# A fused BigBird attention and expert layer on one core: SyncE waits in front of a transfer until most of its older ones have landed

## The chip, the core and the metric

The kernel runs on one core of a Trainium2 chip. The core has five engines that run side by side, each with an instruction queue of its own: TensorE (PE; its weight loads are listed apart as PEld), VectorE (DVE), ScalarE (ACT), GpSimd (POOL) and SyncE (SP). SP does no arithmetic here; it issues transfers, which the core's 16 DMA engines carry out. The metric is the time of one execution on the device in microseconds (us). Times before are the median of three runs. A trace was taken of one more execution; its span is the time from the first to the last recorded instruction.

## The reference

```python
def _attn_ref(q, k, v, sampled_blocks):          # 4 x 8 x 768 x 64, float32
    scores = scale * np.matmul(q, k.transpose(0, 1, 3, 2))
    mask = np.abs(blk_i - blk_j) <= window        # blocks of 32, window 1
    mask = mask | (blk_i == 0) | (blk_j == 0) | (blk_i == n_blocks - 1) | (blk_j == n_blocks - 1)
    for qb in range(n_blocks):
        for kb in sampled_blocks[qb]:             # 3 blocks drawn for each of 24
            mask[qb * block:(qb + 1) * block, kb * block:(kb + 1) * block] = True
    ...
    return np.matmul(attn, v)                     # attn: softmax of the masked scores

def _moe_ref(x, w_in, w_out):                     # 3072 x 512, 512 x 2048, 2048 x 512
    r = np.maximum(x @ w_in, 0.0)
    return (r * r) @ w_out

x = attn_out.transpose(0, 2, 1, 3).reshape(B * S, H * D)
out = _moe_ref(x, w_in, w_out)
```

Attention runs over four batches of eight heads with 768 tokens of 64 numbers. Each token sees its own block of 32, the neighbours, the first and last block, and three blocks drawn at random for its block. The result, 3072 rows of 512, goes through two products with a squared ReLU between them.

## The kernel before

Everything is computed in bf16 with sums in float32. Two heads make a unit, so a batch has four units. **Batches 0 and 1** compute all scores of a unit and multiply by a mask after the exponential. **Batches 2 and 3** (`b >= SB`) compute only what is seen: the queries are taken in visits of two groups, the keys of the drawn blocks are put together by copies (`k_gather`, tile `KG`) and the values are fetched by transfers from a copy of V in device memory (`v_store` writes tensor `rows`, `v_gather` and `v_window` read it into tile `VG`).

For each unit, Q and K are loaded in float32 (`load`, tiles `qs` and `ks`; in batches 0 and 1 as rows of 1536 bytes, in 2 and 3 Q and K as rows of 512 bytes), cast to bf16 (tile `qc`) by DVE or POOL, and turned by a transposing transfer into tile `QKT` (`transp_dma`), which PE reads for the scores. V is loaded (tile `vs`) and cast (tile `VB`). PE multiplies scores into cells of PSUM (`X`), ACT takes the exponential (tile `pT`), DVE masks, PE multiplies with V, DVE normalizes (tile `XS`), and a transposing transfer writes the turned result into tile `xT` (`x_transp_dma`, and `s_transp` in batches 2 and 3). PE multiplies `xT` by `w_in`, DVE, ACT and POOL take the squared ReLU (tiles `r` and `g`), PE multiplies by `w_out`, the result is copied to tile `ys` and stored (`store`).

Nothing here is ordered by a scheduler. About 1220 tasks are made first; then `PROGRAM`, a long string, is read word by word. A word is a letter for the engine (P, V, A, G, S) and the number of a task, and the task's instructions are put at the end of that engine's queue. An engine takes its queue in order. Words of all four batches are mixed, so PE works on the expert product of one batch beside the scores of the next.

SP issues 170 transfers, all on one hardware queue (q1 on the profile's page), in the order of the words that begin with S. Loads of weights and indirect gathers go over POOL's queue (q0). Every transfer of SP signals one of eight semaphores (DMAHW0 to DMAHW7 in the order of instructions), taken in turn, and waits until the transfer that used the same semaphore has landed, so at most eight are under way at once. In the code, SP's transfers are started through the name `sy`, which is `nc.sync`:

Of the kernel before, what the change touches and what calls it, by code (L numbers as in the profile page):

```python
# [12 lines left out]
F32 = mybir.dt.float32  # L13
# [12 lines left out]
def kernel(  # L26
# [11 lines left out]
    nc = tc.nc  # L38
    B, H, S, D = q.shape
# [8 lines left out]
    HP = H // 2  # L48
# [12 lines left out]
    SB, VR, KG_BUFS, VG_BUFS = 2, D + 2, 2, 3  # L61
# [12 lines left out]

    GATES = (4, 5)
    AHEAD = {(2, 4, 9): 2, (3, 0, 1): 0}
    HOLD = {586: 976, 563: 977, 564: 978, 542: 956}
    passed, held_by, last_pe = {}, [None], [None]
    HALVES = slice(0, D), slice(D, P)
    SYNC = mybir.DependencyInfo(mybir.DependencyClass.Sync, mybir.DependencyReason.DATA)  # L80
    MASKED = ((256, 512), (512, 768), (0, 256))
    FULL = (0, 256)
    tasks = []
    class Buf:
        def __init__(self, pool):
            self.pool, self.holds, self.at = pool, 0, None
# [9 lines left out]
    def run_program(bufs):  # L96
        names = {"P": "PE", "V": "DVE", "A": "ACT", "G": "POOL", "S": "SP"}
        taken = {name: [] for name in bufs}
        cells = [None] * NX
        for word in PROGRAM.split():  # L100
            t = tasks[int(word[1:].partition("/")[0])]
            if t.blocks and names[word[0]] in t.blocks[1]:
                wanted[names[word[0]]].append(t.blocks[0])
        for word in PROGRAM.split():
            i, _, spot = word[1:].partition("/")
            t = tasks[int(i)]
            assert not t.done and all(d.done for d in t.deps)
            for b in t.get:
                if b.pool == "X":
                    b.at = int(spot)  # L110
                    old, cells[b.at] = cells[b.at], b
                else:
                    b.at = len(taken[b.pool]) % bufs[b.pool]
                    taken[b.pool].append(b)
                    old = taken[b.pool][-1 - bufs[b.pool]] if len(taken[b.pool]) > bufs[b.pool] else None
                assert old is None or not old.holds
            held_by[0] = passed.get(HOLD.get(int(i)))
            t.fn(names[word[0]])
            passed[int(i)] = last_pe[0]
            t.done = True  # L120
            for b in t.put:
                b.holds -= 1
        assert all(t.done for t in tasks)
# [51 lines left out]
        eng.dma_start(out=raw[u][w][:, :, ns].rearrange("p t n d -> p t (n d)"),  # L175
                      in_=(qv, kv, vv)[w][0, u][:, :, ns.start * D:ns.stop * D])

    sy, sc_ = nc.sync, nc.scalar
    sb_i = consts.tile([nb, n_rand * 2], I32, name="sb_i")
    for eng, u, w, ns in ((sy, None, 0, ALL), (sc_, 0, 1, KEYS[0]), (sy, 0, 0, QRS[0]), (sc_, 0, 1, KEYS[1]), (None, 0, 0, ALL), (sy, 1, 0, QRS[0]),  # L180
                          (sy, 1, 1, ALL), (sy, 2, 0, QRS[0]), (sy, 2, 1, ALL), (sy, 0, 2, ALL), (sy, 3, 0, QRS[0]),
# [43 lines left out]
    col, row = blk[0:nb, 0:nb], blk[0:nb, nb:nb + 1]  # L225
# [346 lines left out]
    def load_blocks(e):  # L572
        if wanted[e]:
            held_at[e].append(blocks_of(wanted[e].pop(0), ENGINE[e]))
# [14 lines left out]
    def k_gather(b, v, g, e):  # L589
# [13 lines left out]
        for r_ in range(RS):  # L603
            eng.tensor_copy(out=rows[:, :, :, r_ * w:(r_ + 1) * w], in_=src[:, :, :, bass.ds(at[r_] * w, w)])  # L604
        for _ in range(AHEAD.get((b, v, g), 1)):
            load_blocks(e)
# [183 lines left out]
    def T_(f, *args, **kw):  # L790
        return Task((lambda e: f(*args, e)), **kw)
# [102 lines left out]
    def visit(b, v, vw, acts):  # L894
        gs_ = [g for g in VISITS[v] if g]
        vb, kb = Buf("vg"), Buf("kg")
        buf_of["vg", b, v] = vb
        cl = T_(v_claim, b, v, get=[vb], deps=mk_claims[-1:])
        parts = [T_(v_gather, b, v, i, deps=vw + [cl, tb["rows"], tb["slots"]]) for i, g in enumerate(VISITS[v]) if g]
        for t_, g in zip(parts, gs_):  # L900
            t_.blocks = g, ("SP",)
        parts.append(T_(v_window, b, v, deps=vw + [cl]))
        kc = {}
        for g in [g for g in VISITS[v] if g]:
            kc[g] = T_(k_gather, b, v, g, get=[] if kc else [kb], deps=[ev[u][1, 0] for u in us] + [tb["slots"], tb["rows"]] + list(kc.values()))
            kc[g].blocks = g, ("POOL", "DVE")
        slots, pts, exs = [], [], []
        for u, _, _, gs in acts:
            xb_, st, pt = Buf("X"), Buf("S"), Buf("pT")
            buf_of["pT", (u, v, gs)] = pt  # L910
            kgs = [kb] if gs[-1] else []
            sc = T_(s_scores, u, v, gs, xb_, deps=[ev[u][1, 0], ev[u][0, 0]] + [kc[g] for g in gs if g], get=[st, xb_], put=kgs)
            sc_of[u].append(sc)
            ex = T_(s_exps, u, v, gs, deps=[sc], get=[pt], put=[xb_, st])
            if gs[-1]:
                ex = T_(s_masks, u, v, gs, deps=[ex] + tb["masks"])
            exs.append(ex)
            pts.append(pt)
        yb, ot, xs = Buf("X"), Buf("po"), Buf("xs")
        va = T_(s_values, b, v, yb, deps=exs + parts + sum((cv[u] for u in us), []), get=[ot, yb], put=pts + [vb])  # L920
        for u in us:
            va_of[u].append(va)
        nm = T_(s_normalize, b, v, deps=[va], get=[xs], put=[yb, ot])
        mu["s", b, v] = T_(s_transp, b, v, deps=[nm] + x_get(b, v // 2 * QW), put=[xs])
# [4 lines left out]
    for i, (c0, c1) in enumerate(((0, QW), (QW, S))):  # L929
        rb_ = Buf("X")  # L930
        t = T_(mask_rows, c0, c1, rb_, get=[rb_])
# [10 lines left out]
    t = T_(table_load, deps=[])  # L942
# [4 lines left out]
    t = T_(table_spread, hb, deps=[tb["slots"]], get=[hb], put=tmp)  # L947
    tb["rows"] = T_(table_rows, deps=[t], put=[hb])
    m_ = [T_(table_masks, g0, g0 + n, deps=[t], put=[hb]) for g0, n in ((0, 6), (6, 5))]
    tb["masks"] = m_  # L950
    for us in [range(b * HP, (b + 1) * HP) for b in range(B)]:
        for u in us:
            prepare(u)
        mine = [a for a in order if a[0] in us]
        if us[0] < HP:
            for c0, c1 in MASKED:
                for n in range(0, NCH, 2):
                    mb = Buf("X")
                    t = T_(mask_tile, n, c0, c1, mb, get=[mb], deps=mr)
                    x = T_(mask_evac, n, c0, c1, deps=[t, mk_claims[[m_[0] for m_ in MASKED].index(c0)]], put=[mb])  # L960
                    for c in range(c0, c1, P):
                        mk[n, c] = mk[n + 1, c] = x
        if us[0] >= SB * HP:
            b = us[0] // HP
            vw = [T_(v_store, b, i, deps=sum((cv[u] for u in us), [])) for i in range(NVS)]
            for v in range(len(VISITS)):
                visit(b, v, vw, [a for a in mine if a[1] == v * P])
            continue
        for a in mine:
            attend(a, us[0] < HP and a[1] == 0)  # L970

    sq_of, gbuf = {}, {}
    for T in TILES:
# [21 lines left out]
        for i, y in enumerate(ys):  # L995
# [10 lines left out]
            yc0 = yc0 or [yc]  # L1006
            T_(store, T, i, y, deps=[yc], put=[ysb])

    PROGRAM = """
        V109 V153 V207 V332 V18 V19 V20 V28 V42 V53 V294 V29 A32 V35 P30/0 P36/1 P0/2 P33/3 V31 V37 A1 P11/0 V34 P100/1 G46  # L1010
        A101 P47/0 P104/2 V43 A105 P44/3 P102/1 V45 V57 V48 P58/2 A103 V54 P111/3 V59 P55/0 P113/2 A112 V56 P115/1 V41 P4/0
# [57 lines left out]
        P17/1 V1212 S1213  # L1069
    """  # L1070
    run_program({"y": 2, "S": 3, "H": 3, "po": 3, "pT": PT_BUFS, "r": R_BUFS, "g": G_BUFS, "ys": YS_BUFS, "qc": QC_BUFS, "xq": XQ_BUFS, "xT": XT_BUFS, "vg": VG_BUFS, "kg": KG_BUFS, "xs": 2, "qs": NRAW, "ks": NRAW - 1, "vs": NRAW - 1})


# [28 lines left out]
```

## Time and the profile before

| | us |
|---|---|
| runs before: median | 256.14 |
| runs before: lowest to highest | 256.11 to 257.24 |
| the profiled execution | 253.89 |
| its span in the trace | 252.1 |

| engine | busy us | instructions |
|---|---|---|
| PE (matmul) | 240.2 | 5265 |
| PEld (weight load) | 180.3 | 5265 |
| ACT | 184.4 | 217 |
| DVE | 164.6 | 386 |
| POOL | 96.5 | 199 |

The page gives the busy time of each engine, then the span in 40 slices, the queues of the DMA engines, the chain of work that ended last, and the costliest groups of instructions. Three lines of its 40 slices tell how the transfers are spread (each digit is a tenth of the slice, a 9 is 90% or more; a slice is 6.3 us):

```profile
PE   7788999999999999899999999899999999999994
...
DMA  6999999999899997999789999992615655242022
GB/s 187 363 291 177 200 246 206 241 254 245 182 276 226 233 243 227 148 271 163 215 235 239 204 203 208 254 270 57 177 30 87 160 156 133 78 127 83 3 86 86
```

PE is busy almost throughout. The DMA engines are full until slice 27, which ends at 170 us, and half empty after that.

### The profile page before, as it was taken

The numbers are of one execution on the slowest core, as the hardware profiler recorded it, in microseconds if no ns is written. First come the engines' busy times: TensorE is split into PE (matmuls) and PEld (weight loads), VectorE is DVE, ScalarE is ACT, GpSimd is POOL, SyncE is SP. The second block draws the span as 40 slices with busy tenths as digits, with TensorE's granted clock in tenths as the row PEclk, the third lists the DMA queues.
The fourth block names the chain that finished last, engine by engine and source line by source line (L and its number), as shares of the span: only waits on it lengthen the run. The fifth ranks groups of instructions, "written<-read, shape, count | busy, mean of one in ns | idle before, by whom it ended". The sixth has DMA issues, their size and how long they took to land.

```text
span 252.1 us, 12049 instructions
## 1 busy us (share of the span) xinstructions
PE 240.2 (95%) x5265; PEld 180.3 (72%) x5265; DVE 164.6 (65%) x386; ACT 184.4 (73%) x217; POOL 96.5 (38%) x199
## 2 busy tenths in 40 slices
PE   7788999999999999899999999899999999999994
PEld 4567889668965678777867776666966774776774
DVE  7668997779799989765653857626466568642300
ACT  3998999999998899868748676778697556225241
POOL 2265634010544014456566934053519306160020
PEclk9999999999999999999999999999999999999999
DMA  6999999999899997999789999992615655242022
GB/s 187 363 291 177 200 246 206 241 254 245 182 276 226 233 243 227 148 271 163 215 235 239 204 203 208 254 270 57 177 30 87 160 156 133 78 127 83 3 86 86
DMA packets 63540, 47.08 MB, mean 187 GB/s; under 512 B 31487, under 2 KB 58496, under 8 KB 63488
## 3 DMA queue, kind: packets, MB, share of 16 engines
q1 hardware_dynamic: 58352, 37.61, 65.2%
q0 software_dynamic: 4448, 8.25, 16.7%
q8 instruction: 41, 0.67, 1.2%
q10 hardware_dynamic: 688, 0.46, 0.6%
q14 instruction: 11, 0.09, 0.1%
HBM read 35.51 MB, written 7.91 MB: 172 GB/s over the span
## 4 chain that ended last, share of the span: by engine, by line
PE 85%; DMA 5%; DVE 4%; issue 2%; POOL 1%; ACT 1%; SPq 1%; DVEq 0%
PE X L209 78%; PE X L660 5%; DMA w_out_sb<-in_moe_w_out_dram 4%; DMA ks<-in_k_dram 2%; PE X L402 1%; DVE pT L371 1%; DVE r L716 1%; POOL g L727 1%; PE X L312 1%; DVE xq L417 1%; DVE qc L129 1%; ACT pT L364 0%; DVE QKT L129 0%; SPq L175 0%; PE X L431 0%
## 5 line engine op out<-in xcount | busy, mean ns | idle before, releaser
L209 PE MATMUL X<-xT,w_in_sb 64*128 64x256 bf16 x1536 | 99.1, 269 | 2.0 <-issue 1.5
L209 PE MATMUL X<-w_out_sb,g 64*128 64x512 bf16 (+3 forms) x960 | 94.6, 333 | 0.5 <-DMA w_out_sb<-in_moe_w_out_dram 0.5
L209 PEld LDWEIGHTS <-w_in_sb 64*128 64x128 bf16 x1536 | 73.5, 94 | 14.3 <-issue 2.6
L364 ACT ACTIVATE pT<-X 128x1024 bf16<-128x1024 f32 x72 | 70.7, 1033 | 6.8 <-PE X L209 5.2
L630 ACT ACTIVATE pT<-X 128x768 bf16<-128x768 f32 (+1 forms) x56 | 41.5, 765 | 25.9 <-PE X L209 24.3
L209 PEld LDWEIGHTS <-g 64*128 64x128 bf16 x960 | 40.5, 94 | 26.7 <-issue 0.6
L725 ACT ACTIVATE g<-r 128x1024 bf16<-128x1024 f32 (+1 forms) x44 | 40.3, 931 | 11.8 <-DVE r L716 11.7
L716 DVE TENSOR_SCALAR r<-X 128x1024 f32<-128x1024 f32 x22 | 26.9, 1223 | 25.1 <-PE X L209 23.6
L371 DVE TENSOR_TENSOR pT<-pT,VG 128x1024 bf16<-128x1024 bf16 x60 | 39.5, 697 | 1.6 <-ACT pT L364 1.4
L727 POOL TENSOR_TENSOR g<-r 128x512 bf16<-128x512 f32 (+1 forms) x16 | 20.7, 1305 | 47.9 <-ACT r L714 23.8
L637 DVE TENSOR_TENSOR pT<-pT,MKS 128x768 bf16<-128x768 bf16 (+1 forms) x48 | 28.3, 618 | 12.2 <-ACT pT L630 11.6
L714 ACT ACTIVATE r<-X 128x1024 f32<-128x1024 f32 x26 | 27.4, 1065 | 10.1 <-PE X L209 9.8
L209 PE MATMUL X<-QKT 64*128 64x256 bf16 (+1 forms) x384 | 31.4, 250 | 0.7 <-DVE QKT L129 0.4
L583 POOL DMA_INDIRECT VG<-rows,idx x20 | 20.3, 1015 | 26.2 <-PE X L209 11.9
L209 PEld LDWEIGHTS <-QKT 64*128 64x128 bf16 x384 | 17.0, 95 | 5.9 <-issue 1.5
L129 POOL CAST VB<-vs 128x768 bf16<-128x768 f32 x10 | 8.4, 847 | 25.6 <-DMA vs<-in_v_dram 24.1
L209 PEld LDWEIGHTS <-pT 64*128 64x128 bf16 x768 | 15.6, 94 | 2.9 <-PE X L209 0.2
L209 PE MATMUL X<-VB,pT 64*128 64x65 bf16 x768 | 17.1, 190 | 0.1
L129 POOL CAST qc<-ks 128x384 bf16<-128x384 f32 (+1 forms) x17 | 8.7, 541 | 20.6 <-DMA ks<-in_k_dram 14.1
L209 PEld LDWEIGHTS <-KG 64*128 64x128 bf16 x528 | 13.3, 95 | 4.2
L660 PEld LDWEIGHTS <-pT 128*64 128x64 bf16 x624 | 11.7, 111 | 4.9 <-issue 4.4
L604 POOL COPY KG<-QKT 128x64 int32 x72 | 15.0, 254 | 0.0
(104 smaller groups left out, 199.0 us busy)
## 6 DMA issues: line engine op xcount, KB each, us to landing
vs<-in_v_dram SPq DMA_DIRECT2D x14, 384.0 KB
ks<-in_k_dram SPq DMA_DIRECT2D x13, 384.0 KB
qs<-in_q_dram SPq DMA_DIRECT2D x12, 384.0 KB
out_dram<-ys SPq DMA_DIRECT2D x9, 512.0 KB
VG<-rows SPq DMA_DIRECT2D x20, 132.0 KB
w_in_sb<-in_moe_w_in_dram POOLq DMA_DIRECT2D x2, 1024.0 KB, 9.7
w_out_sb<-in_moe_w_out_dram POOLq DMA_DIRECT2D x4, 512.0 KB, 10.3
rows<-VB SPq DMA_DIRECT2D x4, 396.0 KB
```

What stands on the lines that cost most here:

```text
L129: (V if e == "DVE" else G).tensor_copy(out=out, in_=in_)
L209: last = nc.tensor.matmul(out(r ^ crossed), lhsT(r ^ crossed, rows), rhs(r ^ crossed, rows), skip_group_check=True, **kw)
L364: A.activation(out=pT[:, :, 0:n], in_=stile.pop(a)[:, :, 0:n], func=AF.Exp, scale=scale)
L371: V.tensor_tensor(out=pT, in0=pT, in1=m[:, None].broadcast_to([P, 2, len(cs), w]), op=AOP.mult)
L583: G.indirect_dma_start(out=to[0:RS * HB], out_offset=None, in_=pairs, in_offset=bass.IndirectOffsetOnAxis(ap=idx[0:RS * HB, g - 1:g], axis=0))
L630: A.activation(out=pT[:, :, 0:n], in_=stile.pop((u, v, gs))[:, :, 0:n], func=AF.Exp, scale=scale)
L637: V.tensor_tensor(out=pT, in0=pT, in1=m[:, None].broadcast_to([P, 2, n]), op=AOP.mult)
L660: nc.tensor.matmul(po[i * D:(i + 1) * D, h, a * VW:(a + 1) * VW], pts[g][:, h, c * D:(c + 1) * D], val, start=a == 0 and c == 0, stop=c == ...
L714: A.activation(out=to, in_=src, func=AF.Relu)
L716: V.tensor_scalar(out=to, in0=src, scalar1=0.0, scalar2=None, op0=AOP.max)
L725: A.activation(out=g, in_=r, func=AF.Square)
L727: (G if e == "POOL" else V).tensor_mul(out=g, in0=r, in1=r)
```

## The change

`sy` becomes an object that keeps a list of the transfers it has sent and their costs. The cost of a transfer is its number of rows times (`ROW_COST` + bytes of a row), with `ROW_COST` 1000. Ahead of each new transfer it counts back from the last one sent, as long as the sum of costs stays at or below `UNDER_WAY`, 1,900,000. What is older than that must have landed: SP gets a no-operation that waits for the landing of the newest of those older ones. This is switched on at the first word of SP whose task belongs to batch 2 or 3 (`third`), which is the 35th of SP's transfers, issued at 56 us in the trace before, and stays on. The order of tasks doesn't change, nor does any instruction of PE, DVE, ACT and POOL.

```diff
+    ROW_COST, UNDER_WAY = 1000, 1900000
...
+            sy.on = sy.on or (word[0] == 'S' and t in third)
             t.fn(names[word[0]])
...
-    sy, sc_ = nc.sync, nc.scalar
+    class Paced:
+        def __init__(self):
+            self.sent, self.landed, self.on = [], 0, False
+
+        def dma_start(self, out, in_, **kw):
+            row = (D * 2 if kw else in_.shape[-1]) * (4 if in_.dtype == F32 else 2)
+            cost = math.prod(in_.shape) // (D * 2 if kw else in_.shape[-1]) * (ROW_COST + row)
+            under_way, k = 0, len(self.sent)
+            while k > self.landed and under_way + self.sent[k - 1][1] <= UNDER_WAY:
+                k -= 1
+                under_way += self.sent[k][1]
+            if self.on and k > self.landed:
+                tc.add_manual_dep(nc.sync.nop().ins, self.sent[k - 1][0], SYNC, reason="little is under way when the next transfer begins")
+                self.landed = k
+            i = nc.sync.dma_start(out=out, in_=in_, **kw)
+            self.sent.append((i.ins.name, cost))
+            return i
+
+    sy, sc_ = Paced(), nc.scalar
...
+        if us[0] == SB * HP:
+            first = len(tasks)
...
+    third = set(tasks[first:])
```

The first place is SP's queue from 95 to 108 us of the trace before, between the load of a Q and the load of a V; a transfer is shown with what it writes and reads, and in brackets what it waits for. Before:

```order
L157 DMA qs_76<-in_q_dram 128x6x128 [waits DMAHW0_49]
L155 DMA vs_79<-in_v_dram 128x2x384 [waits DMAHW1_49,DVE_49]
L541 DMA rows_70<-VB_189 64x3168 [waits DMAHW2_49,Pool_49]
L541 DMA rows_70<-VB_189 64x3168 [waits DMAHW3_49]
L319 DMA_TRANSPOSE QKT<-qc_107 128x6x128 [waits DMAHW4_49,PE_49]
L319 DMA_TRANSPOSE QKT<-qc_109 128x6x128 [waits DMAHW5_49,PE_49,Pool_49]
L319 DMA_TRANSPOSE QKT<-qc_108 128x6x128 [waits DMAHW6_49]
L319 DMA_TRANSPOSE QKT<-qc_106 128x6x128 [waits DMAHW7_49,DVE_49]
L155 DMA vs_80<-in_v_dram 128x2x384 [waits DMAHW0_49]
```

The same rows of the change (all of SP's transfers have the line of the new class):

```order
L194 DMA qs_76<-in_q_dram 128x6x128 [waits DMAHW5_49,DMAHW0_49]
L194 DMA vs_79<-in_v_dram 128x2x384 [waits DMAHW1_49,DMAHW6_49,DVE_49]
L194 DMA rows_70<-VB_189 64x3168 [waits DMAHW2_49,DMAHW7_49,Pool_49]
L194 DMA rows_70<-VB_189 64x3168 [waits DMAHW0_49,DMAHW3_49]
L194 DMA_TRANSPOSE QKT<-qc_107 128x6x128 [waits DMAHW4_49,DMAHW1_49,PE_49]
L194 DMA_TRANSPOSE QKT<-qc_109 128x6x128 [waits PE_49,DMAHW5_49,DMAHW2_49,Pool_49]
L194 DMA_TRANSPOSE QKT<-qc_108 128x6x128 [waits DMAHW4_49,DMAHW6_49]
L194 DMA_TRANSPOSE QKT<-qc_106 128x6x128 [waits DMAHW7_49,DMAHW5_49,DVE_49]
L194 DMA vs_80<-in_v_dram 128x2x384 [waits DMAHW6_49,DMAHW0_49]
```

Nothing moves; every row has one semaphore more. The transfers of these rows signal DMAHW0 to DMAHW7 and then DMAHW0 again, in their order, so the transpose of `qc_108` now also waits for the landing of the one of `qc_107`, two rows above it.

The second place is SP's queue from 136 to 147 us of the trace before, transposes and loads for batch 3. Before:

```order
L319 DMA_TRANSPOSE QKT<-qc_108 128x6x128 [waits DMAHW4_49]
L157 DMA ks_78<-in_k_dram 128x6x128 [waits DMAHW5_49,Pool_49]
L319 DMA_TRANSPOSE QKT<-qc_106 128x6x128 [waits DMAHW6_49]
L157 DMA qs_76<-in_q_dram 128x6x128 [waits DMAHW7_49]
L319 DMA_TRANSPOSE QKT<-qc_109 128x6x128 [waits DMAHW0_49]
L673 DMA_TRANSPOSE xT_117<-XS 128x4x128 [waits DMAHW1_49,DVE_49]
L155 DMA vs_80<-in_v_dram 128x2x384 [waits DMAHW2_49]
```

And of the change:

```order
L194 DMA_TRANSPOSE QKT<-qc_108 128x6x128 [waits DMAHW0_49,DMAHW4_49]
L194 DMA ks_78<-in_k_dram 128x6x128 [waits DMAHW5_49,DMAHW1_49,Pool_49]
L194 DMA_TRANSPOSE QKT<-qc_106 128x6x128 [waits DMAHW4_49,DMAHW6_49]
L194 DMA qs_76<-in_q_dram 128x6x128 [waits DMAHW5_49,DMAHW7_49]
L194 DMA_TRANSPOSE QKT<-qc_109 128x6x128 [waits DMAHW6_49,DMAHW0_49]
L194 DMA_TRANSPOSE xT_117<-XS 128x4x128 [waits DMAHW1_49,DMAHW7_49,DVE_49]
L194 DMA vs_80<-in_v_dram 128x2x384 [waits DMAHW2_49]
```

From the third row on, each transfer but the last also waits for the landing of the one two rows above it; the load into `vs_80` keeps the wait it had.

## The prediction

> **What bounds the kernel now.** I read the page first: the busy shares, the table of DMA queues, and the shares of the chain that ended last.
>
> ```profile
> span 252.1 us, 12049 instructions
> ...
> PE 240.2 (95%) x5265; PEld 180.3 (72%) x5265; DVE 164.6 (65%) x386; ACT 184.4 (73%) x217; POOL 96.5 (38%) x199
> ...
> q8 instruction: 41, 0.67, 1.2%
> ...
> PE 85%; DMA 5%; DVE 4%; issue 2%; POOL 1%; ACT 1%; SPq 1%; DVEq 0%
> ```
>
> TensorE (PE) is busy for 95% of the span, and 85% of the chain is PE. A change that touches only SyncE (SP) can therefore win nothing but time in which PE stands still. Where that is, the windows say; pacing begins with the transfer that SP issues at 56 us, so I cut there.
>
> ```profile
> 57.50:110.00 52.50, 51.51 (x1179) 39.84 (x1176) 46.54 (x112) 47.71 (x52) 16.19 (x30) 1.00 1.05 224
> 110.00:162.30 52.30, 50.00 (x1154) 37.24 (x1154) 30.79 (x75) 36.77 (x46) 30.62 (x71) 1.00 1.07 221
> 175.00:252.00 77.00, 73.80 (x1596) 53.60 (x1590) 35.99 (x74) 40.08 (x51) 24.07 (x38) 1.00 0.38 99
> ```
>
> A row holds the stretch and its length, then the busy time of PE, PEld, DVE, ACT and POOL, the clock, the share of the DMA engines and GB/s. PE stands still for 0.99 us in the first stretch and 2.30 in the second, with the DMA engines full (1.05, 1.07). After 175 us the share is 0.38, and nothing there can be late for want of a place in the queue. The chain of waits says what stopped PE.
>
> ```profile
> 103.04 0.91 issue
> ...
> 109.96 0.50 ACT pT L630
> ...
> 142.48 0.56 issue
> ...
> 149.49 0.48 issue
> ...
> 161.44 0.77 issue
> ```
>
> Four stops of 0.91 + 0.56 + 0.48 + 0.77 = **2.72 us** lie on the chain as "issue": PE waited for nothing that the profile records. Nearly all that PE lost between 57.5 and 162.3 us is these four and the 0.50 behind ACT.
>
> What they are is seen by counting. PE and PEld ran 10530 instructions, and the instruction queue q8 brought 41 packets in 0.67 MB: one packet for each 257 or so. So I counted PE + PEld up to nine moments, from the start.
>
> ```profile
> 0.00:96.81 96.81, 91.38 (x1997) 70.47 (x1999) 80.65 (x191) 87.14 (x98) 32.31 (x62) 1.00 1.06 234
> 0.00:136.73 136.73, 129.90 (x2889) 100.40 (x2891) 105.49 (x249) 117.75 (x135) 53.09 (x121) 1.00 1.04 230
> 0.00:141.34 141.34, 134.51 (x3017) 104.41 (x3019) 108.93 (x260) 121.46 (x139) 57.53 (x129) 1.00 1.05 230
> 0.00:155.47 155.47, 147.59 (x3272) 113.81 (x3273) 118.26 (x278) 129.73 (x149) 65.10 (x142) 1.00 1.06 227
> 0.00:103.94 103.94, 97.61 (x2140) 75.76 (x2140) 87.13 (x203) 94.14 (x106) 32.92 (x63) 1.00 1.06 235
> 0.00:143.03 143.03, 135.64 (x3032) 105.18 (x3032) 109.51 (x261) 121.46 (x139) 59.22 (x136) 1.00 1.04 228
> 0.00:149.97 149.97, 142.10 (x3159) 110.08 (x3159) 114.42 (x272) 126.12 (x145) 62.58 (x139) 1.00 1.06 228
> 0.00:162.21 162.21, 153.57 (x3415) 118.33 (x3416) 122.80 (x292) 134.86 (x155) 66.99 (x144) 1.00 1.06 228
> 0.00:184.09 184.09, 175.45 (x3909) 134.46 (x3911) 133.49 (x327) 151.03 (x174) 77.00 (x171) 1.00 1.02 221
> ```
>
> The four stops end at counts 4280, 6064, 6318 and 6831, which are 184, 176, 174 and 175 above a multiple of 256 (some records are missing). All four stand at the same place of a block of 256 instructions: PE waits for its own code. At 184.09 us, in the quiet part, the count is 7820, or 140 above a multiple. PE passed about that place (156, 148, 148 and 145 above) ahead of the stops at 96.81, 136.73, 141.34 and 155.47 us. The DMA view tells when the packets came; here are the first and last of the four, searched in 0.1 to 0.2 us, and the quiet one at 184.0 to 184.2.
>
> ```profile
> q8 instruction: 1, 0.02, 29.1%
> ...
> q8 instruction: 1, 0.02, 88.4%
> ...
> q8 instruction: 1, 0.02, 29.5%
> ```
>
> The four began at about 101.5, 140.4, 146.7 and 158.3. So in the quiet part the packet comes as PE passes the place (lag about 0), and ahead of the stops it came 4.7, 3.7, 5.3 and 2.8 us later. PE runs on 2.5, 2.6, 3.3 and 3.9 us after the packet began. Had each begun by 0.9, 0.6, 0.5 and 0.8 us sooner, no stop were left.
>
> How deep the queue in front of such a packet is, SP's and POOL's timelines tell.
>
> ```profile
> 108.73 0.54 SPq L157 DMA_DIRECT2D ks<-in_k_dram  x1
> ...
> 116.33 0.96 POOL L129 CAST qc<-ks 128x384 bf16<-128x384 f32 x2 [1.40 <-DMA ks<-in_k_dram]
> ...
> 130.85 2.18 SPq L319 DMA_TRANSPOSE QKT<-qc  x1
> ...
> 163.58 2.79 SPq L673 DMA_TRANSPOSE xT<-XS  x1
> ...
> SPq L1097 <- DMA out_dram<-ys: 1.7, 1, 1.7
> ```
>
> A load of K issued at 108.73 is awaited until 116.33: 7.60 us, where the last store of the kernel, alone, takes 1.7. From 130.85 to 163.58 SP issued 24 transfers, 32.73 / 24 = 1.36 us each. 7.60 / 1.36 = 5.6 transfers are in the queue.
>
> **The change part by part.** *The wait.* A transfer costs its rows x (1000 + row bytes); SP waits until the older ones not yet landed cost 1.9 million at most. By the code a QKT transpose costs 128 x 6 x (1000 + 256) = 964,608, a load in 512-byte rows 1,161,216, one in 1536-byte rows 649,216, a store 780,288. Two transposes make 1.93 million, so only one of these stays under way beside the new one; of load and transpose two stay. From 5.6 the queue falls to two or three, an estimate of 2.7 to 4.1 us at 1.36 each, about half of 7.60. If the lag of a code packet falls in the same ratio, by 2.3, 1.8, 2.6 and 1.4 us, each stop has more than it needs. The term is **-2.72**, bounded by 0 (the lag doesn't hang on SP's queue) and by -3.22 (the 0.50 behind ACT goes too, as the K copies get their transposes sooner). I take -2.72: the rows that it rests on are the stops themselves.
>
> One rule speaks for less. The Trainium skill ("Runtime: NRT & Kernel Launch", "Instruction fetch mechanics") says code is refilled in blocks of 256 instructions, and that crossing a block costs little and is mostly hidden. The block agrees with the 41 packets here; the hiding doesn't, at these four crossings. By that rule the term were 0 and the time 256.1.
>
> *What the waits hold back.* Behind a waiting SP instruction stand all later loads, transposes, gathers and stores, in the order of the program: POOL and DVE wait for loads (casts), PE for QKT and xT. While the queue is never empty, the wait only moves a transfer's waiting from the queue into SP, and costs 0. When one short transfer is left under way, the queue can run empty: a new transpose needs its issue and its travel.
>
> ```profile
> 97.67 9.74 SPq L319 DMA_TRANSPOSE QKT<-qc  x4
> ...
> 114.93 3.69 SPq L444 DMA_TRANSPOSE xT<-XS  x2
> ...
> 170.72 1.20 SPq L673 DMA_TRANSPOSE xT<-XS  x1
> 110.85 0.41 POOL L598 COPY KG<-QKT 128x256 int32<-128x256 int32 x1
> 121.64 1.47 PE L209 MATMUL X<-xT,w_in_sb 64*128 64x256 bf16 x24
> ```
>
> Issue 1.20 + travel 1.7 - the 1.36 of the transfer before = a gap of up to 1.5 us each time. The room: the four QKT transposes issued from 97.67 end at 107.41, POOL's copies of K read them at 110.85, 3.44 later, 1.7 more than the travel. The second half of xT has left SP at 118.62 and PE reads that tile at 121.64: 3.02 later, 1.3 more than the travel. Both are needed sooner by up to 0.91 us once the stop at 103.04 is gone: what is late next is the K copies, ahead of the 0.50 behind ACT, and this xT. The cost lies between 0 and 3.0 (a full gap on the path at both). No row shows such a gap, since the queue was full; nearest is the room, which holds all but 0.2 of one gap at the xT and all but the 0.91 that PE comes sooner at both. I take **+1.0**, about that 0.91 once and a little of a gap; both ends stay in the range.
>
> *The wait instructions.* By the order, 85 rows of SP carry one wait more, each by a no-operation ahead of the transfer. SP takes 1.36 us for a transfer whose issue alone can take 0.54 (the load of K above): it stands in front of full queues, and that waiting hides the no-operations: 0. Uncovered, an instruction without a transfer costs no more than that 0.54. *After 175 us* the older ones have landed when SP comes to the next (the share is 0.38): 0.
>
> Sum: -2.72 + 1.0 = **-1.72**. The profiled execution took 253.89 us (252.1 of span and 1.8 around it) and would take 252.2. The median of the runs lies 2.25 above that execution; taken over as a difference, 256.14 - 1.72 = **254.4**.
>
> **The rivals.** *All of it (B).* The gaps find room everywhere: -2.72 gives 253.4, with the 0.50 also gone 252.9. For it: no engine but PE is on the chain for long. Against it: PE comes sooner at places with 1.3 to 1.7 us of room.
>
> *No change (C), 256.1.* The code packet's lag is not made by SP's queue, or half the queue is deep enough. What would make it so here: q8 shares the DMA engines with q1 packet by packet, and it waits for one packet of each queue, however many stand behind. At 0.67 MB in 41 packets against a full q1 this is a fixed price, and the pacing changes nothing, as the engines stay full. For it: at 158.3 the lag is 2.8 us though POOL's gathers are under way too. Against it: lags of 2.8 to 5.3 us are two to four whole transfers of 1.36, not a packet. The Trainium skill ("DMA: Bandwidth & Descriptors", "Queues, rings and completion order") has this rule: an engine takes turns between queues at packets. The lags of this trace don't agree with it. That the waits bind too seldom also ends here: against it stands that 5.6 transfers are more than 1.9 million holds of any mixture of loads and transposes.
>
> *Slower (D).* The limit is too low for QKT transposes: with two at 1.93 million each waits for the one but one before, and every one of the four from 97.67 loses a gap. 4 x 1.5 = 6.0, less 1.7 of room = 4.3 late at the K copies, of which PE sees all; with the stops gone, 4.3 - 2.72 = +1.6, so 257.7. It decides from a gap of (2.72 + 1.7) / 4 = 1.1 us per transpose on. For it: PE has 95% and no slack to give. Against it: the transposes' issue alone fills 9.74 / 4 = 2.4 us each now, so SP's issue runs beside the landing of the one before.
>
> **How the numbers follow.** Forecast (-0.9 to -2.4): 0.50. B: 0.13. C: 0.21. D: 0.16. The range takes in B and C whole and most of D: 253.0 to 257.4, leaving out some 0.15 of the chance. This kernel can be told from no change from about 0.5%, 1.28 us. Faster by more: all of B and four fifths of the forecast, 0.53. Within: C, a fifth of the forecast, a little of D: 0.33. Slower by more: 0.14.
>
> **What would show it.** Right: "issue" on PE's chain between 57 and 163 us falls from 2.72 to under 0.7, the packets of q8 begin within 3 us of the place 150 above a multiple of 256, loads land in 3 to 4 us, the share of the DMA engines stays above 0.95. The 1.0 shows as new stops of PE behind QKT, KG or xT. Wrong: the four stops stay while landing is shorter (C), or DMA share in 57 to 163 us falls below 0.9 and PE waits for K copies or xT (D). I would be wrong altogether if stops came at other blocks: PE passes a boundary every 6 us, and only 4 of the 18 in (1179 + 1176 + 1154 + 1154) instructions are late now.

## The result, and the profile after

| | us |
|---|---|
| before, median of 4 runs | 256.40 |
| the change, median of 4 runs | 277.58 (273.23 to 279.40) |
| ratio, with its 95% interval | 1.071 (1.060 to 1.083) |
| the change's profiled execution | 279.40, span 277.6 |

The change makes the kernel 7% slower. In every ratio of this document, runs that lie more than 1.5% above the fastest run of their kernel are left out (they form a slower state), while the medians are of all runs: here the ratio compares 276.44 and 273.23 with the four runs before, a difference of some 18 us. The traces below are of single executions, 279.40 beside 253.89 before, so their difference, 25.5 us of span, is larger than that.

Of the page of the change, these are the lines that answer to those of before: busy time, the queue of the code packets, and the chain.

```profile
span 277.6 us, 12092 instructions
...
PE 248.8 (90%) x5265; PEld 188.2 (68%) x5265; DVE 165.4 (60%) x386; ACT 184.4 (66%) x217; POOL 97.6 (35%) x199
...
q8 instruction: 41, 0.67, 1.0%
...
PE 40%; DMA 15%; issue 3%; SPq 2%; DVE 1%; another core or an unknown queue 1%; ACT 1%; POOL 1%; DVEq 0%; POOLq 0%
```

PE has the same 5265 instructions. The span grew by 25.5 us: PE's idle time from 11.9 to 28.8 (+16.9), its busy time by 8.6. The chain of the change could be followed back only to 97.81 us, so its shares, which are of the whole span, add up to some 64%. From there to the end PE has 63% of the chain and DMA 23%; before, over the same part, PE had 98% and DMA nothing. The windows of the change (length, busy time of PE, PEld, DVE, ACT, POOL, granted clock, DMA share, GB/s):

```profile
57.50:110.00 52.50, 46.36 (x1009) 36.28 (x1005) 41.79 (x94) 41.90 (x45) 13.73 (x19) 0.97 0.78 188
110.00:162.30 52.30, 44.45 (x985) 33.73 (x979) 24.89 (x62) 31.23 (x39) 28.94 (x75) 0.97 0.86 180
162.30:201.00 38.70, 30.72 (x627) 21.62 (x623) 17.71 (x60) 21.24 (x27) 10.44 (x24) 0.91 0.77 168
201.00:277.60 76.60, 73.08 (x1570) 53.00 (x1564) 35.04 (x65) 39.22 (x50) 23.93 (x37) 1.00 0.37 99
```

The DMA share fell from 1.05 to about 0.8, and the busy stretch of the DMA engines, which was over by 175 us, now lasts to about 201. Behind it the rest takes the same 77 us as before. What PE and SP wait for, of the change, is told by the table of waits (us in total, times, longest):

```profile
PE X L229 <- DMA xT<-XS: 12.1, 3, 7.3
PE X L229 <- DMA QKT<-qc: 2.1, 1, 2.1
...
PE X L680 <- issue: 1.7, 3, 0.7
...
SPq L192 <- DMA QKT<-qc: 12.0, 7, 3.0
...
SPq L192 <- DMA qs<-in_q_dram: 8.2, 4, 4.6
```

Line 192 is the new no-operation. PE, which waited for no transfer of SP before, now waits 14.2 us for transposes into xT and QKT; SP waits in front of the next transfer while the DMA engines are not full (0.78 and 0.86). A piece of the change's chain shows how (start, length, what):

```profile
110.24 5.45 DMA QKT<-qc
115.68 0.02 issue
115.70 0.02 SPq L192
115.72 0.03 issue
115.75 4.20 DMA QKT<-qc
119.95 0.02 issue
119.96 0.02 SPq L192
```

A transpose is issued at 110.24 and has landed 5.45 later; only then the no-operation ends, and the next but one goes out and takes 4.20. Landing and issue have become one chain.

### The profile page after: what moved, and what is told of

The parts are those of the page before. It is cut to its first block, busy times and chain, and to the rows that moved or that the text cites. A ratio compares the mean times of both kernels' runs of the same rounds, so it can differ in the third digit from the quotient of the medians.

```text
span 277.6 us, 12092 instructions
## 1 busy us (share of the span) xinstructions
PE 248.8 (90%) x5265; PEld 188.2 (68%) x5265; DVE 165.4 (60%) x386; ACT 184.4 (66%) x217; POOL 97.6 (35%) x199
## 4 chain that ended last, share of the span: by engine, by line
PE 40%; DMA 15%; issue 3%; SPq 2%; DVE 1%; another core or an unknown queue 1%; ACT 1%; POOL 1%; DVEq 0%; POOLq 0%
PE X L229 37%; DMA QKT<-qc 8%; DMA xT<-XS 4%; PE X L680 3%; DMA qs<-in_q_dram 2%; SPq L194 2%; ACT pT L650 1%; DVE MKS L131 1%; POOL qc L131 0%; POOL VB L131 0%; DVE pT L391 0%; DVE ys L131 0%; DVE rs L434 0%; DVE idx L546 0%
## 5 line engine op out<-in xcount | busy, mean ns | idle before, releaser
L229 PE MATMUL X<-xT,w_in_sb 64*128 64x256 bf16 x1536 | 103.0, 276 | 13.0 <-DMA xT<-XS 12.1
L229 PEld LDWEIGHTS <-w_in_sb 64*128 64x128 bf16 x1536 | 77.4, 96 | 25.0 <-issue 11.2
L745 ACT ACTIVATE g<-r 128x1024 bf16<-128x1024 f32 (+1 forms) x44 | 40.4, 933 | 11.9 <-DVE r L736 11.8
L391 DVE TENSOR_TENSOR pT<-pT,VG 128x1024 bf16<-128x1024 bf16 x60 | 40.1, 706 | 2.3 <-ACT pT L384 1.1
L657 DVE TENSOR_TENSOR pT<-pT,MKS 128x768 bf16<-128x768 bf16 (+1 forms) x48 | 27.0, 595 | 19.4 <-ACT pT L650 19.0
L747 POOL TENSOR_TENSOR g<-r 128x512 bf16<-128x512 f32 (+1 forms) x16 | 20.7, 1306 | 48.5 <-ACT r L734 24.7
L229 PE MATMUL X<-QKT 64*128 64x256 bf16 (+1 forms) x384 | 33.1, 257 | 4.7 <-DMA QKT<-qc 2.1
L229 PEld LDWEIGHTS <-QKT 64*128 64x128 bf16 x384 | 18.0, 97 | 10.3 <-issue 6.0
L131 POOL CAST qc<-ks 128x384 bf16<-128x384 f32 (+1 forms) x17 | 9.6, 592 | 30.5 <-DMA ks<-in_k_dram 19.6
L131 POOL CAST VB<-vs 128x768 bf16<-128x768 f32 x10 | 9.0, 902 | 30.7 <-DMA vs<-in_v_dram 30.6
L229 PE MATMUL X<-QKT,KG 64*128 64x64 bf16 x528 | 15.3, 192 | 2.1 <-POOL KG L624 1.2
L680 PEld LDWEIGHTS <-pT 128*64 128x64 bf16 x624 | 12.3, 111 | 7.1 <-issue 4.8
```

The lines of the kernel that those rows point to most:

```text
L131: (V if e == "DVE" else G).tensor_copy(out=out, in_=in_)
L229: last = nc.tensor.matmul(out(r ^ crossed), lhsT(r ^ crossed, rows), rhs(r ^ crossed, rows), skip_group_check=True, **kw)
L391: V.tensor_tensor(out=pT, in0=pT, in1=m[:, None].broadcast_to([P, 2, len(cs), w]), op=AOP.mult)
L657: V.tensor_tensor(out=pT, in0=pT, in1=m[:, None].broadcast_to([P, 2, n]), op=AOP.mult)
L680: nc.tensor.matmul(po[i * D:(i + 1) * D, h, a * VW:(a + 1) * VW], pts[g][:, h, c * D:(c + 1) * D], val, start=a == 0 and c == 0, stop=c == ...
L745: A.activation(out=g, in_=r, func=AF.Square)
```

## The experiments

The theory after the result, A: the limit leaves too few transfers under way to keep the queue q1 full; each transfer then costs more of q1's time, and q1 bounds the kernel from 56 to 172 us. The rivals: the wait instructions cost by themselves (B); the loss sits at the four QKT transposes, as the prediction's rival had it; the waits only move the queue into SP, at no cost.

**Waits without effect.** The same no-operations, waiting for an older transfer:

```diff
-tc.add_manual_dep(nc.sync.nop().ins, self.sent[k - 1][0], SYNC, ...)
+tc.add_manual_dep(nc.sync.nop().ins, self.sent[min(k - 1, len(self.sent) - 9)][0], SYNC, ...)
```

> The same waits stand ahead of the same transfers, but for the landing of the ninth transfer back at the latest, which has landed already when SP comes to them. Theory A (the queue runs dry, because too few transfers are left under way, and q1 moves less per us): nothing is held back, so 255.8 to 257.0, the four stops of PE for code are still there with about 2.7 us in sum, the DMA share between 57 and 162 us is 1.05. Theory B (a wait instruction on SP costs by itself, 85 times some 0.2 us, whatever it waits for): 270 or more.

Ratio 0.998 (0.993 to 1.003), median 254.65 beside 253.75 of before on that chip. B is out: the wait instructions stand where they stood in the change, and they cost nothing.

**Other limits.** Only the number changes:

```diff
-    ROW_COST, UNDER_WAY = 1000, 1900000
+    ROW_COST, UNDER_WAY = 1000, 1950000
```

> UNDER_WAY 1,950,000 in place of 1,900,000, by which two QKT transposes (1.93 million) may stay under way beside a new one. Theory A: the gaps around the transposes of QKT shrink by a third to a half, those around loads stay: 264 to 273 where the change took 277.6. Theory B: 277 as before. If the time stays at 277 the transposes are not where the queue runs dry.

Ratio 1.085 (1.074 to 1.096), median 274.46 against 253.75. The median lies just above what A expected (264 to 273), and that on a chip where the kernel before is faster too: as a ratio it is no better than the change (1.071), against A. That two transposes of QKT just exceed 1.9 million is not what decides.

> UNDER_WAY 2,900,000: three transposes of QKT, or two with a load and a half, stay under way. Theory A: the queue runs dry at few places, 256 to 261, and the stops of PE for code are half gone. Theory B: 277, as the number of wait instructions is the same.

Ratio 1.021 (1.012 to 1.030), median 257.36 against 253.75. Some 70% of the loss is gone, as A expected.

> UNDER_WAY 3,800,000, twice the change's. Theory A: the queue never runs dry, so at worst the time of before, 256.4; if fewer transfers in front of a code packet still help, 254.5 to 256. Theory B: 277, as the number of wait instructions is the same.

Ratio 0.998 (0.993 to 1.003), median 253.69. At twice the limit there is no loss, and no gain. (At 3,400,000, below, 1.005.)

**The number under way.** Two older ones left, whatever they cost; for three it is a 3, and for none UNDER_WAY is 0 and the costs stay as they were:

```diff
-    ROW_COST, UNDER_WAY = 1000, 1900000
+    ROW_COST, UNDER_WAY = 1000, 2
...
-            self.sent.append((i.ins.name, cost))
+            self.sent.append((i.ins.name, 1))
```

> UNDER_WAY 0: from the third batch on one transfer at a time. Theory A, now with a size: what q1 moves in a us is what is under way divided by the time that a transfer takes alone; alone a transfer takes 2.4 to 3.5 us by the trace of the change (an xT issued at 100.31 has landed 2.4 later), so the 90 transfers that took 1.36 us each take about 3.2: 256 + 90 x 1.8 = 420 us. A rival, that the waits only move the same queue into SP (the prediction's reason for a cost of 0): no more than the change, 280.

459.91 us in one execution, where before took 257.92. A's 420 was too low: it slowed 90 transfers only, and those behind them were slowed too (last row of the table below). The chain of this run shows each transfer alone:

```profile
132.31 2.75 DMA QKT<-qc
135.06 0.02 issue
135.07 0.02 SPq L192
135.09 0.03 issue
135.12 3.33 DMA ks<-in_k_dram
...
142.17 2.40 DMA xT<-XS
...
147.74 4.08 DMA qs<-in_q_dram
```

From issue to landing these took 2.4 to 4.1 us, and the others on the chain between 60 and 317 us 2.0 to 4.6, where 1.28 us per transfer passed before. The Trainium skill ("DMA: Bandwidth & Descriptors", "Anatomy of one DMA — SWDGE (gpsimd) path") puts a fixed cost of about 2.0 us beside the bytes, for another issuing path; the 2.4 of the smallest transpose here agrees in size.

> Two older transfers may stay under way beside the new one, whatever they cost. Theory A: three under way, at a landing time of some 4 us 1.33 to 1.5 us each: ratio 1.00 to 1.05. The rival, that it is the kinds (transposes held behind each other) and not the number: the ratio stays at 1.07 or above, since the change too leaves one to three under way.

Ratio 1.078 (1.065 to 1.091), median 276.75 against 257.92. A expected at most 1.05; this result is the one that the rival named, by which the kinds count and not the number. The next run holds the same kinds back, with one more left under way, and the one with all transposes free stands further below: by these two the number counts, three under way don't fill q1, and A's size was off.

> Three older transfers may stay under way beside the new one. Theory A: four are enough to keep q1 full: ratio 0.99 to 1.01, and PE's stops for code shrink, as fewer than the 5 to 6 transfers of before stand in front of a code packet.

Ratio 1.030 (1.021 to 1.039), median 264.12. Four under way are better than three, but not enough, against A's 0.99 to 1.01. The DMA share doesn't show what is missing: it is 1.05 between 57.5 and 175 us here, at 211 GB/s where before had 219.

What the runs have in common shows in SP's timeline: the issue of transfer 34, the first that is paced, and of transfer 118, an xT, 84 transfers later. The first pair is of the change, the second of the run with none left, the third of the limit 2,900,000:

```profile
57.72 0.37 SPq L194 DMA_DIRECT2D ks<-in_k_dram  x1
...
189.82 1.21 SPq L194 DMA_TRANSPOSE xT<-XS  x1
...
60.21 0.37 SPq L194 DMA_DIRECT2D ks<-in_k_dram  x1
...
316.91 1.23 SPq L194 DMA_TRANSPOSE xT<-XS  x1
...
55.99 0.37 SPq L194 DMA_DIRECT2D ks<-in_k_dram  x1
...
165.90 2.59 SPq L194 DMA_TRANSPOSE xT<-XS  x1
```

| kernel | 84 transfers, us | each | span | span - issue of transfer 118 |
|---|---|---|---|---|
| before (56.23 to 163.58) | 107.4 | 1.28 | 252.1 | 88.5 |
| limit 2,900,000 | 109.9 | 1.31 | 253.3 | 87.4 |
| three left (59.99 to 172.65) | 112.7 | 1.34 | 261.9 | 89.3 |
| two left (57.9 to 182.4) | 124.5 | 1.48 | 273.3 | 90.9 |
| limit 1,950,000 (57.9 to 185.1) | 127.2 | 1.51 | 269.9 | 84.8 |
| the change | 132.1 | 1.57 | 277.6 | 87.8 |
| none left | 256.7 | 3.06 | 458.1 | 141.2 |

Save for the run with none left, whose gathers after transfer 118 go one at a time too, the end follows the issue of transfer 118 by 85 to 91 us. The time of the kernel is, within some 3 us, the time that these transfers take to be issued plus a constant. The change pays 1.57 - 1.28 = 0.29 us for each of 84: 24.7 us of the 25.5 between these two executions. The table places the loss ahead of transfer 118; it doesn't show by itself that q1 makes it. In the profiled execution of the waits without effect, in which PE stood still for longer (see the end), the 84 transfers took 116.5 us and the rest 87.7. What tells the change from that one is the DMA share between 57.5 and 162.3 us (0.78 and 0.86, against 1.06 and 1.02) and that PE waits for transposes.

**Where the loss sits.** First all transposes freed from waiting:

```diff
-            if self.on and k > self.landed:
+            if self.on and k > self.landed and not kw:
```

> UNDER_WAY 1,900,000 as in the change, but a transpose never waits; loads, gathers and stores do. Theory A with the loss spread over all kinds: 59 waits of 85 stay, ratio 1.02 to 1.05. If the loss sits at the transposes (the prediction's rival, two transposes at 1.93 million): ratio below 1.01. If it sits at the loads: 1.06 to 1.08 as before.

Ratio 1.057 (1.046 to 1.068), median 272.39. Some 80% of the loss stays when no transpose waits, more than the 1.02 to 1.05 expected of an even spread. Loads, gathers and stores held back are enough to make most of it; how much falls to each kind isn't shown.

Then the change's limit only at the four QKT transposes; in the two halves the bounds are 34 to 72, and 73 to the end:

```diff
-            if self.on and k > self.landed:
+            if 66 <= len(self.sent) < 73 and k > self.landed:
```

> UNDER_WAY 1,900,000 only ahead of the transfers 66 to 72: the four transposes of QKT that the prediction's rival priced, a load of V, of Q and of K; six waits. By the rival's price (1.5 us at each of four) 257 to 258 where before takes 254: ratio 1.012 to 1.016. By the trace of the change, where PE fell 3.1 us further back between 107 and 124 us, and by 1.57 against 1.28 us for each of seven transfers (2 us): 1.006 to 1.012. If the loss is only made by the whole queue and not at a place: 1.000.

Ratio 0.9994 (0.996 to 1.003), median 255.56 against 255.26: nothing, where the prediction's rival priced 4.3 us of lateness. The waits did hold: in this trace two of them kept SP for 2.0 us behind a transpose. A few waits at one place are absorbed.

> UNDER_WAY 1,900,000 only ahead of the transfers 34 to 72 of SP (56 to 109 us before). In the change SP was 16.1 us late at transfer 73 and PE 10 to 12 us. If the queue is full behind this stretch and can't win back what it lost: +7 to +12, ratio 1.03 to 1.05. If loads are made so far ahead that the loss is absorbed, as the six waits were: below 1.01.

Ratio 1.045 (1.039 to 1.051), median 268.19 against 257.06: +11.1.

> UNDER_WAY 1,900,000 from transfer 73 on (109 us before, to the end). In the change SP lost 8.6 us more between transfers 73 and 118, and PE 13 us. If the loss is a sum over stretches: +6 to +12, ratio 1.025 to 1.045, and the two halves together make the change's 1.07. If it needs a late first half: below 1.01.

Ratio 1.032 (1.027 to 1.037), median 264.67: +7.6. Together 7.6% where the change has 7.1%. The loss is a sum over stretches; a first half that fell behind is not won back, though nothing paces the transfers after it. In the trace of the second half PE waits only 0.2 us for a transpose by name, and 5.4 us are "issue". The longest of these, 2.45 us from 160.10, stands ahead of products with xT, and SP issued a transpose into xT at 159.06: probably it is a wait for that transpose which the profile doesn't name. This isn't shown.

**A limit that wins?** Three runs looked for the gain without the loss. The first frees the transposes at 2,900,000, the second paces only transfers 92 to 108 at 2,900,000 (`if 92 <= len(self.sent) < 109 and k > self.landed`), the third sets 3,400,000 throughout.

> UNDER_WAY 2,900,000, and a transpose never waits. The trace at 2,900,000 lost 2.5 us around the K copies at 106 to 115 and 2.0 at 154 to 163, both behind transposes that had waited, and got back about 3.6 us of stops for code. Theory A with the number under way near that of before (4.2): ratio 0.990 to 1.005. If the loads alone make the queue too short: 1.01 to 1.03.

0.995 (0.987 to 1.003), from two of the twelve runs; the median of all twelve is 257.54, against 255.26. No gain.

> UNDER_WAY 2,900,000 only ahead of the transfers 92 to 108 of SP (issued from 128 to 150 us before), where the trace at 2,900,000 lost nothing and two stops for code went: ratio 0.992 to 0.998. If the stops for code aren't made by what stands in the queue, 1.000.

0.9952 (0.9906 to 0.9998); but the medians of all twelve and 35 runs stand the other way, 256.22 and 255.26. I don't count it as a gain.

> UNDER_WAY 3,400,000, between the one that lost 2% and the one that lost nothing. Theory A: ratio 0.997 to 1.010, with no better point between. If a limit exists that beats before, it is here or in the run with free transposes: below 0.995.

1.005 (1.001 to 1.010). No limit tried makes the kernel clearly faster.

## Why the prediction was wrong, step by step

**What bounds the kernel: half right.** PE's 95% was read as the only bound, and the DMA share of 1.05 only as a reason why packets are late. Both were full to 162 us. A change on SP could win nothing but PE's idle time, as said; it could lose all that it takes from q1, which was not said.

**The stops for code (-2.72): not shown.** At 2,900,000, where PE's pace is that of before, the table of PE's waits has no "issue" any more, and the chain runs without a stop through the places where before stopped at 142.48 and 149.49:

```profile
141.33 8.29 PE X L229 x144
149.62 0.88 PE X L680 x47
150.50 6.89 PE X L229 x120
```

That run took 1.2 us longer in span all the same: the 2.72 came back as new waits of PE, among them these two.

```profile
PE X L229 <- DVE pT L657: 1.9, 1, 1.9
...
PE X L229 <- POOL KG L624: 1.2, 1, 1.2
```

So the forecast's picture, stops gone and their gain given back, is what this one execution shows, at a limit half again as high. That the shorter queue took the stops away is not shown. The run with waits at the four transposes only has no stop at these two places either, though nothing was held back there. And with the change's own limit a stop can stay; these are PE's waits in the run of the second half:

```profile
PE X L229 <- issue: 3.6, 5, 2.5
...
PE X L680 <- issue: 1.8, 3, 0.8
```

The longest stop of the second row, 0.84 us from 166.85, ends at a count of PE + PEld of 6828, 172 above a multiple of 256: it is the fourth stop of before (0.77 us, at 6831). In the change 1.7 us of "issue" remain at products with VG. Two of these three stops end at 5551 and 5559, 175 and 183 above a multiple of 256, but the last packet of q8 ahead of them had begun by 141.5 us, 4.6 us before the first; their cause stays open. That shorter queues bring the code packets sooner was not tried by itself: every run that shortened the queue moved the other transfers as well.

**What the waits hold back (+1.0, at most 3.0): this step failed.** It said that "while the queue is never empty, the wait only moves a transfer's waiting from the queue into SP", priced a gap of 1.5 us, and counted it at two tight places. The price of one landing was not far off: issue and travel made 2.9, and transfers alone took 2.4 to 4.1. The count was wrong. "From 5.6 the queue falls to two or three" is itself the loss: with so few under way q1 runs dry again and again, and 84 transfers pay 0.29 us each. PE's waits for transposes alone make 14.2 us in the change, where the term was bounded by 3.0. Even "two or three" was too many in part: the prediction has "of load and transpose two stay", but by its own costs a load in 512-byte rows and a transpose of QKT make 2.13 million, so beside a new transfer only one of such a pair stays. A row that spoke for this was quoted: 7.60 us of landing at 1.36 us per transfer was read as a queue that is longer than need be; part of that length is what keeps the engines fed.

**The slower rival (D, 257.7): right in sign, wrong in place and size.** It put the loss at the four transposes and made the limit of 1.93 million decide. Six waits there cost nothing, and the limit of 1,950,000 didn't lower the ratio. It had 0.16 and should have been priced over the whole queue: transfers between 56 and 164 us, times the difference between what each takes with two or three under way and 1.28. The prediction did name D's signs, a DMA share below 0.9 and PE waiting for xT, and these are what came.

**The wait instructions, and the part after 175 us (0): right.** The waits without effect cost nothing, and behind transfer 118 the change takes 87.8 us where before took 88.5.

## What to carry to other kernels

Before transfers are held back, work out how many must be under way. The time that one takes alone, divided by the time per transfer that the queue reaches, is the least that it can be. Here that gives 3 / 1.3 = 2.3, and it was too few: with three under way the kernel lost 8%, with four 3%. Where the DMA share is 1 over the same stretch in which the bounding engine is at 95%, there are two bounds, and any time taken from the queue must be counted over all its transfers, not at the tight places alone. A wait that costs nothing at one place can cost 7% at eighty-five.

## What was not expected of the hardware

**The granted clock was lower where PE paused long.** It was 1.00 throughout before, 0.91 in the change from 162 to 201 us, where PE was busy for 79%, and 0.75 from 60 to 317 us in the run with none left, where it was busy for 52%; that run's PE took 269.2 us for the instructions that took 240.2. Busy time alone doesn't set it: in the run of the second half PE was busy for 78% of 160 to 175 us, at a clock of 1.00. How much of the change's 8.6 us more of busy time lies on the path wasn't separated. But the loss doesn't need the clock: the profiled execution of the second half had 1.00 throughout and a span 7.3 us above that of before.

**The stops for code differ between executions.** The profiled execution with waits that have no effect took 263.14 us, 8.5 over the median of its runs, and has three long stops at the same place of a block; its chain has

```profile
104.60 2.23 issue
...
142.12 1.49 issue
...
148.66 3.79 issue
```

where before had 0.91, 0.56, 0.48 and 0.77. The counts of PE + PEld at their ends are 4284, 5811 and 6065, or 188, 179 and 177 above a multiple of 256. Beside the waits without effect the program is that of before, so the length of these stops is not set by the program alone. They make 7.5 us here against 2.72, more than half of what this execution lies above its median, and a profile of one execution gives the price of these stops only for that execution.
